# Attention feeding a mixture of experts: query chunks of 512, 512, 320 and 512, and a new place for the first block's join

## The chip, the cores and the metric

The kernel runs on one core of one Trainium2 chip. The metric is the device time of one execution in microseconds (us); less is better. The core's engines are the matrix engine PE (its weight loads are shown apart as PEld), the vector engine DVE, the scalar engine ACT, GpSimd (POOL) and SyncE (SP), which here issues nearly all DMAs in one queue, in order. Each engine also works in order.

## The reference

Attention without softmax over 8 batches of 1856 rows is followed by a mixture of 16 experts, in which each row goes to one expert:

```python
scores = scale * np.matmul(z, z.transpose(0, 2, 1))   # z: (8, 1856, 64), scale = 1/1856
attn = np.maximum(scores, 0.0) ** 2
x = u * np.matmul(attn, v)                             # u, v: (8, 1856, 256)
...
g_logits = x @ w_group                                 # 4 groups, the best one is taken
e_logits = xg @ w_expert[g]                            # 4 experts in it, the best one is taken
h = np.maximum(xg[mask_e] @ w1[g, e], 0.0)             # 256 -> 1024
ye = h @ w2[g, e]                                      # 1024 -> 256
out[tok_idx] = combined[:, None] * ye                  # weight of group times weight of expert
```

All data are fp32. The kernel splits each operand into a high and a low part and adds three products, so a "product" below is up to three matmuls.

## The kernel before, in words

**Attention.** A batch's 1856 queries are cut into four chunks of `QW` = 512, 512, 416 and 416 columns, beginning at `QO`. For each chunk there are 15 key steps (14 of 128 keys and one of 64). A step is named (batch, chunk, key step) here, so (7,3,4) is the fifth key step of the last chunk of the last batch. `scores` makes two matmuls of the chunk's width into one of three score banks; ACT takes relu (L330) and square (L336; in key steps 4 and 10 ACT squares twice, L333 and L334), DVE rounds to the high part `ah` (L337) and subtracts to the low part `al` (L340). `attn_v` then adds six matmuls of the chunk's width (L357, L358, L360) to two accumulators. `scores` runs five steps (`LEAD`) ahead of `attn_v`.

**End of a chunk.** `chunk_end` multiplies the accumulators with `ut` (`xT`, L378), splits the result into `xh` and `xl` (L379, L380), and copies it in 16-bit planes into `pl` (L398). Four or five steps later SP issues one DMA transpose for each 128 rows of the chunk (`rows<-pl`, L404), PE makes the router's logits (L414, L415), ACT copies them (`lgp`, L419), SP transposes them (`lgx`, L422), and DVE copies them back (`lgf`, L428) and works through the routing in some 25 small instructions, among them `base` (L542), the running count of rows of each expert. All matmuls of routing share one bank, so the logits of a chunk wait until `base` of the chunk before has been read out of it. POOL scatters the rows to a DRAM buffer, `bucket`, one call for each 128 rows (L552). A chunk whose width is no multiple of 128 has a part tile, with copies and memsets of its own.

**Handing over to the experts.** While the last batch runs, SP issues 16 `fill`s (L640, L641): each writes `NPAD` padding rows of 1056 bytes into `bucket` behind the rows that an expert has after (6,2). It reads the place from `cbi`, which DVE writes after that chunk's routing. The scatter of (6,3) comes after all fills. The first expert's weights are loaded at `E0_LOADS` (`raw_e`, L175 and L184) and split at `E0_CUTS` (ACT L179 and L191, DVE L180 and L192). The rows of the first block of 512 are read back from `bucket` at the first step of `X0_LOADS` (`xp`, L696, and `meta`, L699) and joined at `X0_JOINS`: DVE merges `meta` (L725) and copies `xf` (L710), ACT makes `xh_m` (L716), DVE `xl_m` (L718). The second block is loaded at the second step of `X0_LOADS`.

**Experts.** The blocks of up to 512 rows run one after another: `up` (L735 to L737, then L740 on ACT and L741 on DVE) and `down` (L751 to L753), all in an order written out by hand.

**Order.** The tables give program steps in which an instruction is written down. After the first 15 steps, a scheduler with a timeline of its own then orders the attention's instructions on each engine, so an instruction can stand some steps away from its step.

Of the kernel before, what the change touches and what calls it, by code (L numbers as in the profile page):

```python
# [19 lines left out]
P = 128  # L20
# [4 lines left out]
def f32(ap):  # L25
    return ap.bitcast(F32)
# [3 lines left out]
def tile_glu_attn_moe(  # L30
# [12 lines left out]
    B, D, S = uT.shape  # L43
# [7 lines left out]
    NK = NKF + 1  # L51
    assert TAIL == 64 and DQ == 64 and ND == 2 and NE == 16
    NQ = 4
    QW = [512, 512, 416, 416]
    QO = [0, 512, 1024, 1440]
    ZW = [512, 512, 512, S - 1536]
    assert sum(QW) == S
    assert all(cv % 16 == 0 and cv >= 2 * P for cv in caps)
    RW = D + 8
# [10 lines left out]
    ACT_TWICE = (4, 10)  # L70
    NT = 4
    NEARLY = 2
    NPAD = 3 * P
    FRZ = min(512, min(caps[:NEARLY]))
    assert min(caps[:NEARLY]) > FRZ or len(set(caps)) == 1

# [5 lines left out]
    def sb(tag, shape, dt, bufs, name):  # L82
        return pool.tile(shape, dt, tag=tag, bufs=bufs, name=name)

    def cst(name, shape, dt=F32):
        return pool.tile(shape, dt, tag=name, bufs=1, name=name)
# [23 lines left out]
    views = dram_disjoint_views(bucket, B * NQ * NT + NE)  # L110

    padrow = cst("padrow", [P, RW], I32)
# [58 lines left out]
    def load_w(e, wt, piece, name):  # L171

        raw = new_stg(f"raw_{name}_{piece}")
        if piece < 2:
            nc.sync.dma_start(raw, w1[ds(e, 1), piece * P:(piece + 1) * P, :].rearrange("o p f -> p (o f)"))  # L175

            def split():
                hi, lo = wt["h"][piece], wt["l"][piece]
                held(nc.scalar.copy(out=hi, in_=raw))  # L179
                nc.vector.tensor_sub(out=lo, in0=raw, in1=f32(hi))  # L180
        else:
            q = piece - 2
            rv = raw.rearrange("p (a d) -> p a d", d=D)
            nc.sync.dma_start(  # L184
                rv, w2[ds(e, 1), q * 4 * P:(q + 1) * 4 * P, :].rearrange("o (a p) d -> p (o a) d", p=P)
            )

            def split():
                for j in range(2):
                    t = wt["2"][2 * q + j].rearrange("p (a t d) -> p a t d", a=2, t=2)  # L190
                    held(nc.scalar.copy(out=t[:, :, 0, :], in_=rv[:, 2 * j:2 * j + 2, :]))  # L191
                    nc.vector.tensor_sub(out=t[:, :, 1, :], in0=rv[:, 2 * j:2 * j + 2, :], in1=f32(t[:, :, 0, :]))  # L192

        return split
# [84 lines left out]
    def prep_zm(b, c):  # L279
        zm = sb("zm", [P, 512], F32R, 2, f"zm_{b}_{c}")  # L280
        q = QO[c]
        while q < QO[c] + QW[c]:
            n = min(512 * (q // 512 + 1), QO[c] + QW[c]) - q
            z2h, z2l = bz[(b, q // 512)]
            src, dst = slice(q % 512, q % 512 + n), slice(q - QO[c], q - QO[c] + n)
            nc.vector.tensor_copy(out=zm[0:DQ, dst], in_=f32(z2h[0:DQ, src]))
# [33 lines left out]
    def scores(s):  # L320
        b, c, k = steps[s]
        w = QW[c]
        z2h, z2l = bz[(b, k // 4)]
# [22 lines left out]
    def attn_v(s):  # L346
# [6 lines left out]
        for d in range(ND):  # L353
            d0 = (k % 4) * D + d * P
            dsl = slice(d0, d0 + P)
            o = oa[d][:, 0:QW[c]]
            nc.tensor.matmul(o, vl[:, dsl], ah, start=(k == 0), stop=False)  # L357
# [4 lines left out]
    def load_ut(b, c):  # L362
        w = QW[c]
        t = sb("ut", [P, ND, 512], F32, 2, f"ut_{b}_{c}")[:, :, 0:w]
        nc.sync.dma_start(t, uT[b, :, QO[c]:QO[c] + w].rearrange("(d p) q -> p d q", p=P))
        ut[(b, c)] = t

    def chunk_end(s):
# [8 lines left out]
        for d in range(ND):  # L377
# [4 lines left out]
        nc.gpsimd.iota(rows[:, 0:nt, D + 1:RW], pattern=[[P, nt], [0, RW - D - 1]],  # L382
                       base=b * S + QO[c], channel_multiplier=1)
        part = w % P
# [253 lines left out]
    def fill(e):  # L638

        r = nc.sync.value_load(cbi[0:1, e:e + 1], min_val=0, max_val=NROW - NPAD)  # L640
        ins = nc.sync.dma_start(  # L641
            views[B * NQ * NT + e][ds(r, NPAD), :].rearrange("(p t) w -> p t w", p=P),
            padrow.unsqueeze(1).to_broadcast([P, NPAD // P, RW]),
        )
        filled.append(ins)

# [30 lines left out]
    def regs(j):  # L677
        while not is_sorted:
            run_gens(NS, 1)
        if j not in ereg:  # L680
            ereg[j] = nc.sync.value_load(eli[0:1, j:j + 1], min_val=0, max_val=NE - 1)
            rreg[j] = nc.sync.value_load(rli[0:1, j:j + 1], min_val=0, max_val=(NE - 1) * CAPB)
        return ereg[j], rreg[j]
# [20 lines left out]
    def load_rows(i):  # L704
        j, r0, n = blocks[i]
        rows_b[i] = load_x(i, regs(j)[1] + r0, n)
# [14 lines left out]
    def join_block(i):  # L721
        j, r0, n = blocks[i]
        xp, meta = rows_b[i]
        nt = (n + P - 1) // P
        nc.vector.tensor_tensor(  # L725
            out=meta[:, 0:nt, 1], in0=meta[:, 0:nt, 1], in1=none[:, j, r0 // P:r0 // P + nt], op=ALU.max
        )
        yield from join_x(i, xp, n)
# [164 lines left out]
        ("v", 0, (0, 1), (0, 6)), ("v", 1, (0, 7), (0, 12)), ("v", 2, (0, 13), (1, 4)), ("v", 3, (1, 5), (1, 10)),  # L893
        ("z", 0, (1, 7), (1, 13)), ("z", 1, (2, 5), (2, 11)), ("z", 2, (3, 5), (3, 11)), ("z", 3, (3, 6), (3, 13)),
    )
    E0_LOADS = ((1, 4), (1, 5), (1, 10), (1, 14))
    E0_CUTS = ((1, 9), (1, 13), (2, 5), (2, 8))
    E1_LOADS = ((2, 9), (2, 13), (3, 7), (3, 11))
    E1_CUTS = ((3, 6), (3, 9), (3, 13))
    X0_LOADS = ((2, 3), (3, 4))  # L900
    X0_JOINS = ((2, 10), (2, 11), (2, 12))
    xs = []
    x0 = []
    e0_cuts = []
# [2 lines left out]
    def step(s):  # L907
# [8 lines left out]
        if b + 1 == B:  # L916
            if (c, k) in E0_LOADS:
                e0_cuts.append(load_w(regs(0)[0], wts[0], E0_LOADS.index((c, k)), "e0"))
            if (c, k) in E0_CUTS:
                e0_cuts[E0_CUTS.index((c, k))]()  # L920
            if (c, k) in E1_LOADS:
                wts.setdefault(1, {"h": [], "l": [], "2": []})
                e1_cuts.append(load_w(regs(1)[0], wts[1], E1_LOADS.index((c, k)), "e1"))
            if (c, k) in E1_CUTS:
                pc = E1_CUTS.index((c, k))
                add_w(wts[1], pc, "e1")
                e1_cuts[pc]()
            if (c, k) in X0_LOADS:
                load_rows(X0_LOADS.index((c, k)))
            if (c, k) == X0_JOINS[0]:  # L930
                x0.append(join_block(0))
            if (c, k) in X0_JOINS:
                xs[:] = [next(x0[0])]
# [10 lines left out]
        if len(filled) < NE and s == NS - NQ * NK + 1 + len(filled) * 7 // 4:  # L944
            fill(len(filled))
# [226 lines left out]
    with order:  # L1172
        for g in range(NB * NF):
            i, f = divmod(g, NF)
            e, r0, n = blocks[i]
# [26 lines left out]
            if i >= OLD:  # L1202
                if f == 2 and i > OLD:
                    p = i - 1
# [5 lines left out]
        e, r0, n = blocks[i]  # L1210
# [42 lines left out]
```

## Time and profile before

| | |
|---|---|
| median of 3 runs | 1535.82 us (1535.66 to 1537.08) |
| the profiled execution's own time | 1536.54 us |
| its span in the profile | 1534.8 us |
| granted PE clock, mean | 0.997 |
| attention, from the first matmul of `attn_v` to the last | 9 to 842 us |
| matmuls of 512 and of 416 columns in attention | 1888 and 1888 |

Rows of a timeline give the start, the duration, the engine, the line and the tiles of an instruction. In square brackets stands the engine's idle time before it and what ended it. Matmuls overlap: the time that one costs is the distance to the next one's start, not its duration.

### The profile page before, as it was taken

What the parts mean: (1) busy time and instruction counts of PE and PEld (TensorE: products, weight loads), DVE (VectorE), ACT (ScalarE), POOL (GpSimd) and SP (SyncE); (2) the same over time, 40 slices, a digit from 0 to 9 for tenths busy, and PEclk for the clock granted to TensorE, in tenths of its full rate; (3) what the DMA queues carried; (4) which work ended last, traced back from release to release, by engine and by line L of the source; (5) the groups of instructions that cost most, each with busy time, mean ns of one, the idle gap of its engine ahead of it and who ended that gap; (6) DMA issues with size and microseconds to landing.
All of it is one profiled execution on the core that took longest, in us unless ns stands there. A gap on an engine that the chain in (4) does not pass through costs nothing. (4 is left out here: it accounts for less than half of the span.)

```text
span 1534.8 us, 23216 instructions
## 1 busy us (share of the span) xinstructions
PE 1519.0 (99%) x7527; PEld 1338.9 (87%) x7527; DVE 1118.4 (73%) x2676; ACT 999.4 (65%) x1896; POOL 293.5 (19%) x356
## 2 busy tenths in 40 slices
PE   9999999999999999999999999999999999999998
PEld 7898988988989989889888799998888888888887
DVE  7888878888888888788887658765655566666663
ACT  8888788878888888788886444444444444444442
POOL 0013121211221121212112231211221222221112
PEclk9999999999999999999999999999999999999999
DMA  4334333323333243333545344554444445454430
GB/s 136 102 74 126 83 85 104 86 76 102 87 105 84 70 112 84 79 87 87 166 157 120 91 114 116 133 115 125 112 118 115 125 118 133 128 131 126 126 97 30
DMA packets 301995, 163.51 MB, mean 107 GB/s; under 512 B 240027, under 2 KB 283043, under 8 KB 301872
## 3 DMA queue, kind: packets, MB, share of 16 engines
q1 hardware_dynamic: 289568, 130.72, 34.4%
q0 software_dynamic: 11952, 30.90, 6.3%
q8 instruction: 59, 0.97, 0.3%
q14 instruction: 64, 0.52, 0.1%
q10 hardware_dynamic: 352, 0.39, 0.1%
HBM read 72.50 MB, written 38.45 MB: 72 GB/s over the span
## 5 line engine op out<-in xcount | busy, mean ns | idle before, releaser
L740 ACT ACTIVATE hh<-ph 128x512 fp32r<-128x512 f32 (+10 forms) x288 | 156.1, 542 | 349.6 <-PE ph L737 342.9
L357 PE MATMUL o<-ah,vl 128*128 128x512 f32 (+1 forms) x960 | 357.3, 373 | 3.0 <-DVE ah L337 2.8
L358 PE MATMUL o<-ah,vh 128*128 128x512 f32 (+1 forms) x960 | 357.2, 372 | 0.0
L741 DVE SCALAR_TENSOR_TENSOR hl<-ph,hh 128x512 fp32r<-128x512 f32 (+10 forms) x288 | 177.3, 616 | 223.7 <-ACT hh L740 182.5
L340 DVE TENSOR_TENSOR al<-r,ah 128x512 fp32r<-128x512 f32 (+1 forms) x448 | 286.4, 640 | 66.9 <-ACT r L334 49.7
L330 ACT ACTIVATE r<-sc 128x512 f32<-128x512 f32 (+1 forms) x480 | 257.5, 552 | 97.0 <-PE sc L328 83.5
L360 PE MATMUL o<-al,vh 128*128 128x512 f32 (+1 forms) x896 | 281.0, 373 | 0.4 <-DVE al L340 0.4
L336 ACT ACTIVATE r<-r 128x512 f32<-128x512 f32 (+1 forms) x416 | 238.7, 591 | 5.2
L552 POOL DMA_INDIRECT bucket<-rows,di x128 | 138.7, 1083 | 485.3 <-DVE al L340 177.4
L756 POOL DMA_INDIRECT out_dram<-yf,meta x121 | 124.0, 1025 | 511.1 <-DVE yf L795 483.3
L737 PE MATMUL ph<-xl_m,w1h_e 128*128 128x512 f32 (+10 forms) x576 | 208.0, 361 | 0.0
L736 PE MATMUL ph<-xh_m,w1h_e 128*128 128x512 f32 (+10 forms) x576 | 207.8, 361 | 0.0
L735 PE MATMUL ph<-xh_m,w1l_e 128*128 128x512 f32 (+10 forms) x576 | 207.5, 360 | 0.0
L357 PEld LDWEIGHTS o<-ah,vl 128*128 128x128 f32 x960 | 181.1, 189 | 22.8 <-DVE ah L337 3.3
L358 PEld LDWEIGHTS o<-ah,vh 128*128 128x128 f32 x960 | 181.2, 189 | 18.8
L753 PE MATMUL y<-hl,w_e 128*128 128x512 f32 (+9 forms) x544 | 196.3, 361 | 0.3 <-DVE hl L741 0.3
L752 PE MATMUL y<-hh,w_e 128*128 128x512 f32 (+9 forms) x544 | 196.1, 360 | 0.0
L751 PE MATMUL y<-hh,w_e 128*128 128x512 f32 (+9 forms) x544 | 196.0, 360 | 0.0
L360 PEld LDWEIGHTS o<-al,vh 128*128 128x128 f32 x896 | 167.5, 189 | 18.1 <-DVE al L340 1.3
L337 DVE CAST ah<-r 128x512 fp32r<-128x512 f32 (+1 forms) x416 | 168.4, 405 | 19.3 <-ACT r L336 17.8
L327 PE MATMUL sc<-zm,z2h 128*128 128x512 f32 (+1 forms) x480 | 179.7, 374 | 0.8 <-ACT r L330 0.8
L328 PE MATMUL sc<-zm,z2l 128*128 128x512 f32 (+1 forms) x480 | 178.6, 372 | 0.0
(170 smaller groups left out, 2088.9 us busy)
## 6 DMA issues: line engine op xcount, KB each, us to landing
raw_e<-in_w_dram SPq DMA_DIRECT2D x64, 512.0 KB
vr<-in_v_dram SPq DMA_DIRECT2D x23, 512.0 KB
ut<-in_uT_dram SPq DMA_DIRECT2D x16, 512.0 KB
ut<-in_uT_dram SPq DMA_DIRECT2D x16, 416.0 KB
bucket<-padrow SPq DMA_DIRECT2D x16, 396.0 KB
zr<-in_zT_dram SPq DMA_DIRECT2D x47, 128.0 KB
vr<-in_v_dram SPq DMA_DIRECT2D x9, 256.0 KB
rows<-pl SPq DMA_TRANSPOSE x128
```

What stands on the lines that cost most here:

```text
L330: nc.scalar.activation(out=a, in_=ps[:, 0:w], func=AF.Relu, scale=1.0 / S)
L336: nc.scalar.activation(out=a, in_=a, func=AF.Square)
L340: nc.vector.tensor_sub(out=al, in0=a, in1=f32(ah))
L357: nc.tensor.matmul(o, vl[:, dsl], ah, start=(k == 0), stop=False)
L358: nc.tensor.matmul(o, vh[:, dsl], ah, start=False, stop=(k == NK - 1))
L360: nc.tensor.matmul(o, vh[:, dsl], al, start=False, stop=False)
L735: nc.tensor.matmul(o, wt["l"][d][:, fs], xh[:, d, 0:W], start=(d == 0), stop=False)
L736: nc.tensor.matmul(o, wt["h"][d][:, fs], xh[:, d, 0:W], start=False, stop=False)
L737: nc.tensor.matmul(o, wt["h"][d][:, fs], xl[:, d, 0:W], start=False, stop=(d == ND - 1))
L751: nc.tensor.matmul(o, w2t[:, 1, dsl], hh[:, 0:W], start=(f == 0), stop=False)
L752: nc.tensor.matmul(o, w2t[:, 0, dsl], hh[:, 0:W], start=False, stop=False)
L753: nc.tensor.matmul(o, w2t[:, 0, dsl], hl_[:, 0:W], start=False, stop=(f == NF - 1))
```

## The change

The query chunks become 512, 512, 320 and 512 wide. The fills write 416 rows instead of 384, from 104 partitions with four rows each instead of 128 with three. The first expert's third and fourth weight pieces are loaded two and one steps later, and its first, second and fourth piece are split two, one and one steps later. The first block's rows are loaded two steps later and joined in the last chunk, at key steps 3 to 5, instead of the third chunk, at key steps 10 to 12; the second block's rows are loaded four steps later.

```diff
-    QW = [512, 512, 416, 416]
-    QO = [0, 512, 1024, 1440]
+    QW = [512, 512, 320, 512]
+    QO = [0, 512, 1024, 1344]
...
-    NPAD = 3 * P
+    PADP = 104
+    NPAD = 4 * PADP
...
-            views[B * NQ * NT + e][ds(r, NPAD), :].rearrange("(p t) w -> p t w", p=P),
-            padrow.unsqueeze(1).to_broadcast([P, NPAD // P, RW]),
+            views[B * NQ * NT + e][ds(r, NPAD), :].rearrange("(p t) w -> p t w", p=PADP),
+            padrow[0:PADP].unsqueeze(1).to_broadcast([PADP, NPAD // PADP, RW]),
...
-    E0_LOADS = ((1, 4), (1, 5), (1, 10), (1, 14))
-    E0_CUTS = ((1, 9), (1, 13), (2, 5), (2, 8))
+    E0_LOADS = ((1, 4), (1, 5), (1, 12), (2, 0))
+    E0_CUTS = ((1, 11), (1, 14), (2, 5), (2, 9))
...
-    X0_LOADS = ((2, 3), (3, 4))
-    X0_JOINS = ((2, 10), (2, 11), (2, 12))
+    X0_LOADS = ((2, 5), (3, 8))
+    X0_JOINS = ((3, 3), (3, 4), (3, 5))
```

One line more stands ahead of the rest, so L725 of before is L726 of the change, and so on.

What the tables do to the order is seen on the engines. First DVE, around the first block's join. Before, `al_10837` is the low part of step (7,3,1) and `ah_10853` the high part of (7,3,2):

```order
L340 TENSOR_TENSOR al_10837<-r_10832,ah_10834 128x416
L481 TENSOR_TENSOR key_1_10710<-key_1_10710,iota_78 128x80
L725 TENSOR_TENSOR meta_10626<-meta_10626,none 128x4
L487 TENSOR_REDUCE sm_1_10731<-ex_1_10708 128x20
L710 COPY xf_10803<-xp_10624 128x2x2x512
L484 TENSOR_REDUCE km_1_10729<-key_1_10710 128x20
L337 CAST ah_10853<-r_10851 128x416
```

In the change, `al_10798` is the low part of (7,3,3) and `al_10822` that of (7,3,4), whose high part ACT makes:

```order
L341 TENSOR_TENSOR al_10798<-r_10793,ah_10795 128x512
L485 TENSOR_REDUCE km_1_10652<-key_1_10633 128x20
L508 RECIPROCAL sm_1_10654<-sm_1_10654 128x20
L491 TENSOR_TENSOR oh_1_10677<-key_1_10633,km_1_10652 128x80
L726 TENSOR_TENSOR meta_10590<-meta_10590,none 128x4
L711 COPY xf_10906<-xp_10588 128x2x2x512
L497 TENSOR_TENSOR oh_7_1_10680<-oh_1_10677 128x64
L519 TENSOR_TENSOR sel_1_10741<-sm_1_10654,oh_1_10677 128x16
L511 COPY pre_1_10722<-oh_7_1_10680 128x16
L523 TENSOR_REDUCE ew_1_10744<-sel_1_10741 128x4
L515 TENSOR_TENSOR pre_1_10722<-pre_1_10722,oh_7_1_10680 128x16
L341 TENSOR_TENSOR al_10822<-r_10817,ah_10819 128x512
```

The join has moved back by two steps on DVE, and it stands behind `xT` and `xl` of chunk (7,2) instead of ahead of them.

Second, SP's queue where the first block's rows are read back (`lgx_1` and `rows_1` belong to chunk (7,1)). Before:

```order
L422 DMA_TRANSPOSE lgx_1_10562<-lgp_1_10561 128x8x48
L696 ISA
L696 DMA_TRANSPOSE xp_10624<-bucket 128x4x512
L699 ISA
L699 DMA meta_10626<-bucket 128x4x2
L404 DMA_TRANSPOSE rows_1_10558<-pl_1_10560 128x4x128 x4
```

In the change:

```order
L423 DMA_TRANSPOSE lgx_1_10483<-lgp_1_10482 128x8x48
L405 DMA_TRANSPOSE rows_1_10479<-pl_1_10481 128x4x128 x4
L697 ISA
L697 DMA_TRANSPOSE xp_10588<-bucket 128x4x512
L700 ISA
L700 DMA meta_10590<-bucket 128x4x2
```

The four transposes of chunk (7,1) have moved ahead of the two reads.

Third, SP's queue at the first expert's first weights (`raw_e_0`, `raw_e_1`). Before, the last three of the 16 fills stand behind them:

```order
L175 ISA
L175 DMA raw_e_0_10259<-in_w_dram 128x1024
L175 ISA
L175 DMA raw_e_1_10277<-in_w_dram 128x1024
L640 TENSOR_LOAD cbi
L640 ISA x2
L641 ISA
L641 DMA bucket<-padrow 384x1x264
```

In the change the last fill stands ahead of `ut`, of the transposes of chunk (7,0) and of the weights:

```order
L642 DMA bucket<-padrow 416x1x264
L366 DMA ut_2_10033<-in_uT_dram 128x2x320
L405 DMA_TRANSPOSE rows_0_10022<-pl_0_10024 128x4x128 x4
L423 DMA_TRANSPOSE lgx_0_10026<-lgp_0_10025 128x8x48
L682 TENSOR_LOAD eli
L682 ISA x2
L683 TENSOR_LOAD rli
L683 ISA x2
L176 ISA
L176 DMA raw_e_0_10182<-in_w_dram 128x1024
```

So all fills are ahead of the weights. Of the 16, two still stand ahead of the transposes of chunk (6,3) and 14 behind its `lgx`, as a block.

Three more moves are told in words. DVE's `cbi` stands behind `al` of (7,0,4), before it stood behind `ah` of (7,0,7). DVE's `lgf` of chunk (6,3) stands behind `al` of (7,0,10), before behind `al` of (7,0,12), and ACT's exponential of that routing stands ahead of the relu of (7,0,13), before ahead of that of (7,1,0). ACT's split of the first weight piece stands behind the square of (7,2,0), before behind that of (7,1,13).

## The prediction

> **What bounds the kernel now.** I read the page first: which engine fills the span.
>
> ```profile
> PE 1519.0 (99%) x7527; PEld 1338.9 (87%) x7527; DVE 1118.4 (73%) x2676; ACT 999.4 (65%) x1896; POOL 293.5 (19%) x356
> ```
>
> PE is the bound, so an edit pays only if it makes matmuls cheaper or takes a PE wait away. Next the timeline of PE, for starts that lie further apart than one matmul costs. The longest such place is in the last batch, at the first block's join. Rows of PE, DVE, POOL and SP:
>
> ```profile
> 813.26 0.54 PE L360 MATMUL o<-al,vh 128*128 128x416 f32 x2
> 816.20 0.72 PE L357 MATMUL o<-ah,vl 128*128 128x416 f32 x1 [2.40 <-DVE ah L337]
> 819.71 0.35 PE L327 MATMUL sc<-zm,z2h 128*128 128x416 f32 x1
> ...
> 813.91 0.17 DVE L725 TENSOR_TENSOR meta<-meta,none 128x4 int32<-128x4 int32 x1 [1.92 <-DMA meta<-bucket]
> 814.14 1.29 DVE L710 COPY xf<-xp 128x2048 uint16<-128x2048 uint16 x1
> 815.47 0.68 DVE L337 CAST ah<-r 128x416 fp32r<-128x416 f32 x1
> ...
> 802.13 1.01 POOL L552 DMA_INDIRECT bucket<-rows,di  x1 [6.66 <-DVE di L548]
> 809.29 0.17 POOL L382 IOTA rows<- 128x28 int32 x1 [1.37 <-DMA bucket<-rows,di]
> ...
> 804.02 1.23 SPq L422 DMA_TRANSPOSE lgx<-lgp  x1
> 809.32 2.11 SPq L696 DMA_TRANSPOSE xp<-bucket  x1
> 812.11 5.12 SPq L404 DMA_TRANSPOSE rows<-pl  x4
> ```
>
> The scatter of chunk (7,0) lands at 809.3, the reads start there, `meta` lands 4.6 us later, DVE has waited 1.92 us for it, and `ah` of (7,3,2) stands behind the join. PE stands still for 2.4 us. Then it is slow: 10 matmuls fill 816.20 to 819.71, 3.51 us, where 188.3 ns each (below) would make 1.88. The whole place costs 2.56 + 1.63 = 4.2 us.
>
> Two smaller waits stand near: for the first expert's weights, and for the last chunk's logits.
>
> ```profile
> 776.81 0.96 SPq L175 DMA_DIRECT2D raw_e<-in_w_dram  x2
> 780.64 1.05 ACT L179 CAST w1h_e<-raw_e 128x1024 fp32r<-128x1024 f32 x1 [4.79 <-DMA raw_e<-in_w_dram]
> 782.24 0.46 PE L327 MATMUL sc<-zm,z2h 128*128 128x416 f32 x1 [0.83 <-ACT r L330]
> ...
> 847.88 1.28 DVE L192 TENSOR_TENSOR w_e<-raw_e,w_e 128x512 fp32r<-128x512 f32 x2
> 849.52 0.43 PE L414 MATMUL pl<-xh,whl 128*128 128x416 f32 x1 [1.77 <-DVE base L542]
> ```
>
> They cost some 1.0 and 1.9 us. All else is matmul time.
>
> **The change part by part.** *Widths.* First and last rows of runs without a gap: 416 columns in attention (86 matmuls between the starts), 512 in attention (88), 320 in an expert block (71).
>
> ```profile
> 589.22 0.35 PE L327 MATMUL sc<-zm,z2h 128*128 128x416 f32 x1
> 605.41 0.54 PE L360 MATMUL o<-al,vh 128*128 128x416 f32 x2
> ...
> 222.91 0.39 PE L327 MATMUL sc<-zm,z2h 128*128 128x512 f32 x1
> 242.88 0.39 PE L357 MATMUL o<-ah,vl 128*128 128x512 f32 x1
> ...
> 902.75 0.31 PE L735 MATMUL ph<-xh_m,w1l_e 128*128 128x320 f32 x1
> 913.16 0.31 PE L753 MATMUL y<-hl,w_e 128*128 128x320 f32 x1
> ```
>
> That is 16.19/86 = 188.3 ns, 19.97/88 = 226.9 and 10.41/71 = 146.6. Two matmuls of 416 cost 376.6 ns, one of 512 and one of 320 cost 373.5. A chunk has 118 matmuls and 4 of logits, so 8 x 122 pairs save 3.1 ns each: -3.0 us. Ends: 0 (nothing shows 320 columns in attention) and -4.
>
> *Do ACT and DVE keep up at 320 columns?*
>
> ```profile
> L330 ACT ACTIVATE r<-sc 128x512 f32<-128x512 f32 x240 | 138.4, 592 | 51.4 <-PE sc L328 46.2 <-DVE al L340 2.4 <-DVE ah L337 1.0
> L330 ACT ACTIVATE r<-sc 128x416 f32<-128x416 f32 x240 | 119.1, 512 | 45.6 <-PE sc L328 37.3 <-issue 1.4 <-DVE ah L337 1.1
> L337 DVE CAST ah<-r 128x512 fp32r<-128x512 f32 x208 | 88.5, 425 | 9.1 <-ACT r L336 7.8 <-issue 0.6 <-ACT r L330 0.6
> L337 DVE CAST ah<-r 128x416 fp32r<-128x416 f32 x208 | 80.0, 384 | 10.2 <-ACT r L336 10.0
> L340 DVE TENSOR_TENSOR al<-r,ah 128x512 fp32r<-128x512 f32 x224 | 155.0, 692 | 44.6 <-ACT r L334 38.0 <-ACT r L336 3.2
> L340 DVE TENSOR_TENSOR al<-r,ah 128x416 fp32r<-128x416 f32 x224 | 131.4, 587 | 22.3 <-ACT r L334 11.7 <-ACT ah L333 6.6 <-ACT r L336 1.7
> 476.40:499.70 23.30, 23.30 (x126) 22.46 (x125) 18.48 (x57) 19.89 (x40) 5.21 (x7) 1.00 0.33 81
> ```
>
> The last row is an undisturbed chunk of 416, (4,2): 23.3 us, DVE busy for 18.5 and ACT for 19.9. From 512 to 416 columns relu loses 80 ns, the rounding `ah` 41 and `al` 105, so I let them lose as much again to 320. With square like relu, 15 steps take 2.4 us from ACT; 14 `al` and 13 `ah` take 2.0 from DVE. PE's chunk loses about 41.7 ns in 108 matmuls and gains 38.6 in the 10 scores of the next chunk: 19.2 us. ACT would be busy for 17.5 of 19.2 (91%, before 85%) and DVE for 16.5 (86%, before 79%), with the end of a chunk of 512 among it. Score banks and the five steps' lead buffer bursts of some 3 us, so I take no wait of weight: +0.5 us over all batches, ends 0 and +4 (0.5 a batch). The dearer step of 512 in the last chunk has room. Fewer part tiles, memsets and scatters lie beside PE: nothing.
>
> *The join.* The anchors are the first matmul of the last step of chunk (7,1), just behind which chunk (7,2) begins, and the first expert's wait, used further down:
>
> ```profile
> 780.79 0.61 PE L360 MATMUL o<-al,vh 128*128 128x512 f32 x2
> 787.36 0.39 PE L357 MATMUL o<-ah,vl 128*128 128x512 f32 x1
> ```
>
> In the change SP first issues `lgx` of (7,1), then four transposes (5.12 us in the row above), then the reads. Before, `lgx` stood at 804.02, 16.6 us after this anchor; ACT saves up to 2.1 of its 2.4 us by then, so I take 14.5 to 16.6. With 1.2 for `lgx` itself, 5.1 for the transposes and 4.6 up to the landing, `meta` is there 25.4 to 27.5 us after the anchor. PE begins the last step of (7,2) some 19.2 us after the anchor, and is at (7,3,4) another 7.0 us on (four steps of 8 x 226.9 ns are 7.3; the first of them mixes in matmuls of 320): at 26.2. That step's `al` is due four matmuls later, at 27.1. After `meta`, DVE needs 0.1 + 1.2 + 0.5 of routing + 0.6 for that `al`, so it is ready at 27.8 to 29.9. PE waits for 0.7 to 2.8 us; I take 1.3, as ACT's lead makes the earlier end likelier. A wait near the upper end, the length of that before, could bring the slow spell too. Gain 4.2 - 1.3 = -2.9; ends -4.2 and 0. If the reads' cover is gone, `al` of (7,3,4) is late next.
>
> *Weights and fills.* Rows of SP and DVE:
>
> ```profile
> 740.10 0.17 DVE L594 CAST cbi<-base 128x16 int32<-128x16 f32 x1
> 741.33 2.43 SPq L641 DMA_DIRECT2D bucket<-padrow  x2
> 746.93 1.22 SPq L422 DMA_TRANSPOSE lgx<-lgp  x1
> 749.73 0.35 DVE L428 COPY lgf<-lgx 128x320 uint16<-128x320 uint16 x1 [2.07 <-DMA lgx<-lgp]
> 752.55 11.86 SPq L641 DMA_DIRECT2D bucket<-padrow  x9
> 744.56 0.69 DVE L340 TENSOR_TENSOR al<-r,ah 128x512 fp32r<-128x512 f32 x1 [1.57 <-ACT r L336]
> 748.59 0.60 ACT L330 ACTIVATE r<-sc 128x512 f32<-128x512 f32 x1 [0.55 <-PE sc L328]
> q1 hardware_dynamic: 2948, 2.95, 71.5%
> ```
>
> A fill takes 11.86/9 = 1.32 us of SP. The last row is the DMA view of 752 to 764 us (packets, MB, share of 16 engines): 71.5% busy, so a longer fill can hide in SP's spacing up to 1/0.715, and 8% more rows do. `cbi` is ready about two steps earlier less what stands ahead of it, some 1.7 us. SP issues two fills, four transposes and `lgx` by some 749.5, 14 fills by 768.5 to 770.5, `ut`, four transposes, `lgx` and the register loads, and the weights at 777 to 779, before 776.8. They land 3.8 us later, at 781 to 783. ACT splits them two steps later than before, and the score that needs the relu behind them comes at 784.4 instead of 781.2 (where the row of 780.79 ends PE's work before), since in PE's order 12 matmuls of 512 and some of 320 lie between; 1.45 us after the landing is 782.3 to 784.2. So the wait of 1.0 goes: -0.8, ends -1.0 and +1.5.
>
> By the Trainium skill's "DMA: Bandwidth & Descriptors", section on why a DMA increments its semaphore by 16, a transfer uses the largest number of engines up to 16 that divides its outer dimension: 16 for 128 partitions, 13 for 104. By that rule a fill would keep 13 engines busy 416/384 x 16/13 = 1.33 times as long, 1.26 us for 0.94 (0.715 x 1.32), just under the 1.32 of its issue: the sum would stay, and the rival on fills below would be avoided by 5%. The trace does not name a packet's engine.
>
> *A new wait.* `lgf` of (6,3) now stands two steps earlier on DVE, behind `al` of (7,0,10) (the row of 744.56), and the exponential behind it stands on ACT ahead of relu (7,0,13). Before, `lgf` waited for 2.07 us without a wait of PE. Now DVE comes to it at 745.2 and `lgx` lands at 750.4 to 751.2. Relu (7,0,13) can start 2.0 us after the landing and be done 0.6 us later. PE's scores of (7,0,14) end at 748.6, where the ACT row follows them; those of (7,1,1), which need relu (7,0,13)'s bank, come 17 matmuls, 3.9 us, later: 752.5. PE waits for 0.5 to 1.3: +0.8, ends 0 (the cover before was whole) and +2.
>
> *Last chunk's logits.* They wait until `base` of (7,2) is read. The pair of splits (1.28 us) that stood ahead of it now stands before `xT`, and PE has three matmuls more (0.7 us) to do first; the wider `xT` and `xl` take 0.4 longer. Of 1.9 I leave 1.0: -0.9, ends -1.9 and +1.0.
>
> Sum: -3.0 + 0.5 - 2.9 - 0.8 + 0.8 - 0.9 = -6.3 us against the span of 1534.8, which lies 1.7 below that execution's own time of 1536.5, which is 0.7 above the median of 1535.8. So the median comes to 1529.5.
>
> **The rivals.**
> *The join only moves its wait* (no change or little gain): `meta` lands at 27.5 or later, because four transposes now stand ahead of it. PE then waits 2.5 us and runs 1.6 us slow; so the gain of 2.9 is gone down to 0.1; with the widths at nothing besides, -0.5 is left: 1535.3. For it speaks that SP's queue is the longer one; against it that PE needs the rows two steps, 3.6 us, later.
> *The narrow chunk starves* (slower): ACT's relu comes later than the score banks bear, in each batch, from 20.5 us of ACT work in a chunk of 19.2 on. At 20.7, 1.5 us in each of eight batches, this gives +12 for +0.5, so 1529.5 + 11.5 = 1541. For it: the four copies of 1.0 and 0.6 us at a chunk's end come in a row. Against it: 85% busy without a PE gap before.
> *Fills hold the queue*: if a fill's time goes with the rows of one partition, four for three, 1.32 us become 1.76, 14 take 6 us more, `lgx` of (7,0) and the weights land at 787 to 789, and PE waits 4.5 us and runs 1.6 slow: the gain of 0.8 becomes a loss of 6.1, 1529.5 + 6.9 = 1536.4.
> *The widths pay nothing, the waits go*: 1529.5 + 3.0 = 1532.5. For it speaks that no row has 320 columns in attention; against it the straight fall from 226.9 at 512 to 146.6 at 320.
>
> **How the numbers follow.** Forecast 0.56, its own range 1526 to 1532.7; the widths without gain 0.16; the join's wait stays 0.11; fills 0.08; starving 0.09. A measurement tells about 0.2%, 3.1 us, from no change: faster means below 1532.7, slower above 1538.9. Faster: 0.56 + 0.16 = 0.72. Same: 0.11 and 0.08, with rounding 0.18. Slower: about 0.10. The low end takes the gains at their ends without the join's last microsecond, 1525; the high end reaches to the first and third rival, 1536.
>
> **What would show it.** The matmuls of 512 and 320 at 227 and 147 ns in attention, and PE in (4,2) without rows in brackets: the widths. PE at step (7,3,4) with a wait below 2 us, and no slow spell: the join. `raw_e` without a long bracket on ACT that PE repeats: the weights. A bracket on PE near 753: the new wait. The sum is wrong if brackets on PE appear in each batch's third chunk, or if rows of fills stand 1.7 us apart.

## The result, and the profile after

The change makes the kernel slower: 1554.7 us (1553.35 to 1557.8) against 1536.26 in the same comparison, a ratio of 1.0123 with a 95% interval of 1.0105 to 1.014. Forecast were 1529.5 us, a range of 1525 to 1536, and a chance of about 0.10 for slower.

The page's line on the engines, of the change:

```profile
PE 1515.8 (98%) x7527; PEld 1300.2 (84%) x7527; DVE 1119.4 (72%) x2644; ACT 1002.4 (65%) x1872; POOL 276.5 (18%) x332
```

PE works 3.2 us less than before, as the new widths let one expect, in a span of 1551.6 instead of 1534.8. So the loss is a wait. PE's timeline shows it in the second of these rows:

```profile
777.46 0.62 PE L361 MATMUL o<-al,vh 128*128 128x512 f32 x2
799.82 0.80 PE L358 MATMUL o<-ah,vl 128*128 128x512 f32 x1 [21.74 <-DVE ah L338]
800.41 0.63 PE L359 MATMUL o<-ah,vh 128*128 128x512 f32 x1
```

PE stands still for 21.7 us at the end of chunk (7,1), and the next rows come 0.43 us apart for some 3 us, in place of 0.23. The bracket names `ah`; who held it up is seen on DVE, ACT and SP in the same stretch:

```profile
799.10 0.35 DVE L429 COPY lgf<-lgx 128x320 uint16<-128x320 uint16 x1 [22.84 <-DMA lgx<-lgp]
...
800.61 0.44 ACT L331 ACTIVATE r<-sc 128x320 f32<-128x320 f32 x1 [22.99 <-DVE al L341]
...
803.84 1.05 ACT L180 CAST w1h_e<-raw_e 128x1024 fp32r<-128x1024 f32 x1 [2.29 <-DMA raw_e<-in_w_dram]
...
737.10 6.01 SPq L405 DMA_TRANSPOSE rows<-pl  x4
743.21 1.21 SPq L423 DMA_TRANSPOSE lgx<-lgp  x1
745.83 43.29 SPq L642 DMA_DIRECT2D bucket<-padrow  x14
789.22 0.46 SPq L366 DMA_DIRECT2D ut<-in_uT_dram  x1
789.90 6.04 SPq L405 DMA_TRANSPOSE rows<-pl  x4
796.04 1.21 SPq L423 DMA_TRANSPOSE lgx<-lgp  x1
799.45 0.94 SPq L176 DMA_DIRECT2D raw_e<-in_w_dram  x2
```

Read from the bottom: the 14 fills hold SP's queue until 789. Behind them stand the transposes and `lgx` of chunk (7,0) and the first expert's weights. DVE has come to `lgf` of that chunk at 776 and waits there, with the attention's `ah` and `al` behind it in its order; ACT and PE run dry one after the other. Not the weights stop the kernel first, but the router's logits one row ahead of them; the weights cost ACT another 2.3 us.

A fill takes much more of SP than before. The fills' rows among the instructions that touch `bucket`, of before and then of the change (ns shortest, median, longest, then first and last start):

```profile
L641 SPq DMA_DIRECT2D bucket<-padrow x16: 547/554/693, 741.3 to 781.9; - x16
```

```profile
L642 SPq DMA_DIRECT2D bucket<-padrow x16: 953/960/1125, 731.9 to 788.2; - x16
```

The issue itself went from 0.55 to 0.96 us. From 745.83 to the last start at 788.2 the fills stand 3.26 us apart, where 1.32 were expected. Most of the rest is the next fill's register load of `cbi`, which the rows above leave out: in the trace's records it takes 0.3 to 0.4 us behind most fills of before and 1.73 to 1.95 behind a fill here.

And the DMA view of that stretch in the change:

```profile
DMA packets 5579, 5.74 MB, mean 133 GB/s; under 512 B 169, under 2 KB 5577, under 8 KB 5577
q1 hardware_dynamic: 5577, 5.71, 48.8%
```

The 16 DMA engines are busy for 48.8% here, for 71.5% in before's stretch of 752 to 764 us. So the transfers are not at a limit; the time goes on SP itself.

### The profile page after: what moved, and what is told of

It is laid out like the page before. It is cut to its first block, busy times and chain, and to the rows that moved or that the text cites. A ratio compares the mean times of both kernels' runs of the same rounds, so it can differ in the third digit from the quotient of the medians.

```text
span 1551.6 us, 23124 instructions
## 1 busy us (share of the span) xinstructions
PE 1515.8 (98%) x7527; PEld 1300.2 (84%) x7527; DVE 1119.4 (72%) x2644; ACT 1002.4 (65%) x1872; POOL 276.5 (18%) x332
## 5 line engine op out<-in xcount | busy, mean ns | idle before, releaser
L361 PE MATMUL o<-al,vh 128*128 128x512 f32 (+1 forms) x896 | 295.7, 372 | 0.5 <-DVE al L341 0.5
L553 POOL DMA_INDIRECT bucket<-rows,di x120 | 129.3, 1077 | 566.1 <-issue 239.3
```

Of the source, the lines that this page charges most:

```text
L361: nc.tensor.matmul(o, vh[:, dsl], al, start=False, stop=False)
```

## The experiments

The theory after this reading: a fill is dear when its partition count isn't a multiple of 16, whatever it carries. The rival: four rows a partition, or the longer fill, is dear.

**Fills of 128 partitions with four rows.**

```diff
-    PADP = 104
+    PADP = 128
```

> The change with fills of 512 rows from 128 partitions with four rows each (instead of 416 from 104). Theory P (a fill whose partition count is no multiple of 16 is dear; the change's fills stand 3.25 us apart on SP, before's 1.4): though a third more bytes than before are written, the fills stand 1.4 to 1.9 us apart, the first weights land by 785, PE's wait of 21.9 us is gone, and the time is 1529 to 1534. Theory R (four rows a partition, or the longer fill as such, is what is dear): 3.2 us or more apart, PE still waits some 20 us or more, 1555 to 1565.

Measured 1528.65 us (1528.09 to 1531.63, before 1535.49), ratio 0.9957 (0.9944 to 0.9971). One number of the change makes the difference between 18 us lost and 7 gained. SP's queue now, and the DMA view of 743 to 764.4:

```profile
743.09 21.36 SPq L642 DMA_DIRECT2D bucket<-padrow  x14
764.54 0.59 SPq L366 DMA_DIRECT2D ut<-in_uT_dram  x1
765.35 5.51 SPq L405 DMA_TRANSPOSE rows<-pl  x4
770.96 1.21 SPq L423 DMA_TRANSPOSE lgx<-lgp  x1
775.61 0.46 SPq L176 DMA_DIRECT2D raw_e<-in_w_dram  x2
...
q1 hardware_dynamic: 6576, 6.74, 93.4%
```

The fills carry 23% more rows than the change's and are through in half the time, now at the limit of the DMA engines. This is the change as it was meant, and below it is called the mended change.

**Fills of 120 partitions with four rows** (`PADP = 120`).

> The change with fills of 480 rows from 120 partitions with four rows each. Theory P: 120 is no multiple of 16 either, so the fills stand 3.2 to 3.8 us apart (3.25 times 480/416 at most), time 1554 to 1562. Theory R: about 3.2 to 3.8 as well. If only the number of engines counted (15 of 16 for 120, 13 for 104), they would be at 1.9 or less and the time near 1532.

Measured 1557.99 us (one run), fills 3.30 us apart, issue 0.99. 120 partitions are as dear as 104.

**Fills of 32 partitions with thirteen rows** (`PADP = 32`, `NPAD = 13 * PADP`).

> The change with its 416 rows written from 32 partitions with thirteen rows each. Theory P: 32 is a multiple of 16, so the fills stand 1.3 to 1.6 us apart and the time is 1528 to 1533. Theory R: thirteen rows a partition are dearer than four, so 3.2 us apart or more and 1555 or more.

Measured 1539.77 us (1538.47 to 1542.58), ratio 1.0027 (1.0017 to 1.0037): between the two. The issue is cheap again (0.61 us), but the fills stand 2.2 us apart, with the DMA engines 92% busy (746 to 765 us): a packet of 1056 bytes takes 79 ns in the median, where all other forms so far have 47. Neither theory had that: the forecasts were 1528 to 1533 and 1555 or more. PE waits 8.2 us.

**The kernel before with the change's fills.**

```diff
-    NPAD = 3 * P
+    PADP = 104
+    NPAD = 4 * PADP
...
-            views[B * NQ * NT + e][ds(r, NPAD), :].rearrange("(p t) w -> p t w", p=P),
-            padrow.unsqueeze(1).to_broadcast([P, NPAD // P, RW]),
+            views[B * NQ * NT + e][ds(r, NPAD), :].rearrange("(p t) w -> p t w", p=PADP),
+            padrow[0:PADP].unsqueeze(1).to_broadcast([PADP, NPAD // PADP, RW]),
```

> The kernel before, with the change's fills (104 partitions with four rows) and nothing else of it. Theory P and theory R alike: 13 of the 16 fills stand ahead of the first weights, each 1.85 us longer, so the weights land some 20 us later than at 780.6, PE waits some 17 to 21 us near 781, and the time is 1553 to 1558: the fills alone make the whole loss. Rival (the loss comes from all 16 fills now standing ahead of the weights, and from the later table entries): 1536 to 1542.

Measured 1561.61 us (1560.51 to 1562.29), ratio 1.017 (1.0154 to 1.0185). PE waits here too:

```profile
800.99 0.80 PE L358 MATMUL o<-ah,vl 128*128 128x512 f32 x1 [18.07 <-DVE ah L338]
```

The fills alone do the harm, more than forecast, since smaller waits (0.92 at 758, 1.73 at 806) come on top. In this kernel 13 of the 16 stand ahead of the weights, as before; so it is not the cause that all 16 do in the change.

**Fills of 112 partitions with four rows** (`PADP = 112`, seven times 16).

> The change with fills of 448 rows from 112 partitions (7 x 16) with four rows each. Theory P (a count that is no multiple of 16 is dear): the fills stand 1.4 to 1.65 us apart, as with 128 partitions (1.60), and the time is 1527.5 to 1530. Rival (only the full 128 partitions, or a power of two, is cheap): 3.2 us apart, as with 104 and 120, and 1554 to 1558.

Measured 1530.9 us (1529.05 to 1532.87), ratio 0.9971 (0.9961 to 0.9981); fills 1.67 us apart, issue 0.61. So it is the multiple of 16, not the full 128 and not a power of two. The time is a small miss: PE still waits 1.41 us at 778. The 14 fills begin 1.4 us later than with 128 partitions, behind transposes that take 7.45 us instead of 5.90, and stand a little further apart, so `lgx` of (7,0) is issued at 774.36 instead of 770.96. Packets of the fills take 57 ns in the mean here, against 50 with 128 partitions. Why, no run tells.

**Fills of 8 partitions with 52 rows** (`PADP = 8`, `NPAD = 52 * PADP`).

> The change with its 416 rows written from 8 partitions with 52 rows each, so that 8 engines carry a fill. Theory K (any count of engines below 16 costs SP more): the fill's issue takes about 1 us as with 104 and 120 partitions (0.96 and 0.99; 0.55 to 0.61 with 16 engines). Rival (only a count that is no power of two): 0.6 us or less. Either way a fill's transfer itself is longer, 52 rows an engine at 47 to 80 ns, so they stand 2.5 to 4.5 us apart and the time is 1545 to 1575.

Measured 1651.14 us (one run). Packets take 153 ns here, and the fills stand 7.5 us apart, so the forecast of the time missed by far. Only the first fill, which has no other fill ahead of it, tells the theories apart. For each form, from SP's records: the first fill's issue and the register load that follows it, and the mean distance of the last 14:

| fill | rows | first issue, us | register load after it, us | distance, us |
|---|---|---|---|---|
| before, 128 x 3 | 384 | 0.69 | 0.30 | 1.41 |
| 128 x 4 | 512 | 0.70 | 0.30 | 1.60 |
| 112 x 4 | 448 | 0.76 | 0.30 | 1.67 |
| 32 x 13 | 416 | 0.76 | 0.29 | 2.20 |
| 120 x 4 | 480 | 1.16 | 1.97 | 3.30 |
| 104 x 4 | 416 | 1.12 | 1.95 | 3.26 |
| 8 x 52 | 416 | 0.93 | 2.22 | 7.55 |

(Of before, the distance is that of the nine in a row.) In the third and fourth column together there are two groups, with nothing between: from the first fill's start, multiples of 16 leave SP free after 1.0 to 1.1 us, the others after 3.1 to 3.2. A power of two doesn't help: 8 partitions cost as much.

Then the rest of the change. **Only the widths** (the mended change with both of before's tables).

> The kernel before with the new widths and fills of 512 rows from 128 partitions; the tables of the first expert's weights and of the first block's rows are those of before. Widths worth what the prediction gave them (3.0 us, in the long runs 0.34 a batch by now), the join's wait of 4.2 us kept, weights up to 2.6 us later for 13 fills that are 0.2 us longer each: 1532 to 1537, and the time from one batch to the next falls from 102.9 to 102.5 or 102.6. If the narrow chunk starved, brackets on PE would stand in each batch and the time would be above 1538.

Measured 1535.42 us (1535.02 to 1536.56), ratio 1.0004 (0.9995 to 1.0013). The chunks are cheaper, yet the end does not move. PE:

```profile
778.84 0.41 PE L328 MATMUL sc<-zm,z2h 128*128 128x320 f32 x1 [1.84 <-ACT r L331]
780.20 0.81 PE L361 MATMUL o<-al,vh 128*128 128x512 f32 x2 [0.80 <-DVE al L341]
...
810.34 0.42 PE L358 MATMUL o<-ah,vl 128*128 128x320 f32 x1 [2.68 <-DVE ah L344]
```

Chunk (7,0) begins at 726.5 instead of 730.0, and PE then waits for the weights (2.6 us) and at the join (2.7), each with a slow spell behind it. That lies within the forecast of 1532 to 1537.

**The mended change with the old join.**

```diff
-    X0_LOADS = ((2, 5), (3, 8))
-    X0_JOINS = ((3, 3), (3, 4), (3, 5))
+    X0_LOADS = ((2, 3), (3, 4))
+    X0_JOINS = ((2, 10), (2, 11), (2, 12))
```

> The change with fills of 128 partitions (512 rows), but with the first block's rows loaded and joined where before had them (third chunk, key steps 10 to 12). If the move of the join is worth what the prediction said (2.9 us): 1531 to 1533, with a wait and a slow spell of PE early in chunk (7,3). Rival, the move's gain is given back at the last chunk's logits (there 2.6 us of wait and a slow spell follow in the version with the moved join): 1528 to 1530, and the logits wait below 2 us here.

Measured 1532.05 us (1529.77 to 1533.31), ratio 0.9977 (0.9968 to 0.9986; the interval overlaps a little with the mended change's 0.9944 to 0.9971). The time is that of the first theory and the place that of neither: near the join PE waits only 0.7 us, and the price is paid at the last chunk's logits:

```profile
844.00 0.77 PE L415 MATMUL pl<-xh,whl 128*128 128x512 f32 x1 [4.14 <-DVE df L546]
```

**The mended change with the old weights table** (`E0_LOADS`, `E0_CUTS` of before).

> The change with fills of 128 partitions (512 rows), but with the first expert's weights loaded and split where before had them. If moving them is worth what the prediction gave (0.8 us): 1529 to 1530. Rival, from the pair with the old join (1535.4 without and 1532.1 with the move): about 3 us, since the narrower chunk brings PE to the first split's place earlier than in before: 1531 to 1533.5, with a PE wait of 2 to 4 us at 776 to 781 that the version with the move doesn't have.

Measured 1532.3 us (1531.27 to 1533.49), ratio 0.9981 (0.9972 to 0.999), with waits of 2.01 and 0.80 us at 779 and 781 that the mended change doesn't have. The rival was nearer: by the medians the move is worth 3.65 us, not 0.8. The two traces alone don't show it: their spans are 1529.8 here and 1529.9 in the mended change, whose profiled execution (1531.63 us) is the slowest of its five and pays at the last chunk's logits.

**Before with the new join only** (`X0_LOADS`, `X0_JOINS` of the change).

> The kernel before with only the first block's rows loaded and joined where the change has them. If the move of the join is worth the predicted 2.9 us by itself: 1531.5 to 1533, the wait and the slow spell near 815 gone. Rival, it is given back at the last chunk's logits: 1534 to 1536, with a wait there above 2.5 us (before 1.9).

Measured 1534.54 us (1532.22 to 1536.4), ratio 0.9993 (0.9984 to 1.0002). The wait of 2.4 us at the join is gone, but:

```profile
847.25 0.69 PE L414 MATMUL pl<-xh,whl 128*128 128x416 f32 x1 [3.26 <-DVE base L542]
```

The logits wait 3.26 us instead of 1.77, with a slow spell of 5.8 us behind them.

**Before with both tables.**

> The kernel before with both tables of the change (first expert's weights, first block's rows), but with the old widths and the old fills. By the prediction's terms (join 2.9, weights 0.8, logits 0.9, new wait -0.8): 1531 to 1533. Rival, the tables only pay together with the new widths: 1534 to 1537.

Measured 1534.16 us (1533.01 to 1535.26), ratio 0.9991 (0.9982 to 1.0). No wait at the weights, none at the join, and 3.90 us with a spell at the logits. The rival was nearer.

**The mended change with a later second join.** In it, too, the last chunk's logits wait 2.63 us for `base`. DVE's rows show what stands ahead of `base`:

```profile
840.73 0.68 DVE L742 SCALAR_TENSOR_TENSOR hl<-ph,hh 128x512 fp32r<-128x512 f32 x1
841.33 0.15 DVE L726 TENSOR_TENSOR meta<-meta,none 128x4 int32<-128x4 int32 x1
841.40 0.20 DVE L536 TENSOR_TENSOR rk<-pk,base 128x48 f32<-128x48 f32 x1
841.54 1.31 DVE L711 COPY xf<-xp 128x2048 uint16<-128x2048 uint16 x1
842.74 0.20 DVE L541 TENSOR_TENSOR rk<-rk,oh 128x48 f32<-128x48 f32 x1
842.86 0.17 DVE L543 TENSOR_TENSOR base<-pk,base 128x16 f32<-128x16 f32 x1
...
843.17 0.77 PE L415 MATMUL pl<-xh,whl 128*128 128x512 f32 x1 [2.63 <-DVE base L543]
```

`xf` of the second block (1.31 us) stands between, though nobody needs it yet.

```diff
-                f0 = 4 if i + 1 == NEARLY else 3
+                f0 = 4 if i + 1 <= NEARLY else 3
```

> The change with fills of 128 partitions (512 rows), and with the second block's join begun one step of the first block later (as the third block's already is), so that on DVE the base of (7,2) stands ahead of that join's copy xf (1.3 us) instead of behind it. Theory: the logits' wait of 2.63 us near 842 falls to 1.0 to 1.5, the slow spell behind it goes (another 1.9 us), and the time is 1525 to 1527, from 1528.65. Rival: the second block's rows come too late for its first matmuls, PE waits there instead: 1528 to 1530.

Measured 1527.53 us (1525.17 to 1528.49), ratio 0.9944 (0.9931 to 0.9958). The row in its place:

```profile
842.04 0.47 PE L415 MATMUL pl<-xh,whl 128*128 128x512 f32 x1 [1.42 <-DVE df L546]
```

The wait is down by 1.2 us and the slow spell gone; the profiled spans are 1529.9 and 1526.7. The medians differ by 1.1 us only, less than forecast, and the two intervals overlap: that this wait is shorter is shown by the trace, that this version is the faster one is not settled by the times. Both beat before and the change.

## Why the prediction was wrong, point by point

*Fills: the step that failed.* The prediction let 14 fills take 1.32 us of SP each and said that 8% more rows hide in the spacing. They took 3.26. (Its 1.32 is a little low even for before: the row of 11.86 us ends with the ninth fill's issue, and from start to start it is 1.41.) It bounded the cost by rows and by the share of the DMA engines, the two things that the fill of before shows; what SP itself spends on a fill was taken as fixed, and before has fills of one partition count only. The rival "fills hold the queue" had the mechanism and the place (`lgx` of (7,0) and the weights), but its price came from rows a partition (1.76 us) and it got 0.08. Its 6 us of delay would be 27 with the measured distance.

By the Trainium skill's "DMA: Bandwidth & Descriptors", section on why a DMA increments its semaphore by 16, 104 partitions go to 13 engines. The trace agrees: packets of 4 bytes come 16 a fill before (128 from 753 to 766 us, in which eight fills end) and 13 a fill in the change (169 for thirteen). The cost that the prediction drew from it, 16/13 on the transfer, was the wrong one: 120 partitions, on 15 engines, are as dear as 104. The same section says that the issuing sequencer writes the increments of the unused engines itself; that would fit a cost on SP, though not in proportion: 1, 3 and 8 such writes go with register loads of 1.97, 1.95 and 2.22 us. What SP does in that time, no run shows.

*Widths (-3.0): right in the batches, lost at the end.* One batch that nothing disturbs, (4,0) to (4,3), in windows of before and then of the change (busy us of each engine; a row gives its window and length first):

```profile
sum 102.90, PE 102.90 PEld 90.79 DVE 83.28 ACT 85.89 POOL 19.48; mean PE 25.73 PEld 22.70 DVE 20.82 ACT 21.47 POOL 4.87
```

```profile
474.40:494.50 20.10, 20.10 (x128) 19.14 (x128) 16.43 (x51) 18.29 (x41) 4.84 (x6) 1.00 0.43 99
...
sum 102.60, PE 102.60 PEld 86.14 DVE 85.84 ACT 86.23 POOL 17.50; mean PE 25.65 PEld 21.54 DVE 21.46 ACT 21.56 POOL 4.38
```

That is 0.30 us a batch, 2.4 in eight. Matmuls of 320 stand 146.7 ns apart in attention (46 in 377.66 to 384.26), as in the experts' blocks. The narrow chunk, the row of 474.40, has ACT busy for 18.29 of 20.10, 91% as worked out, and DVE for 82% (86% forecast); no batch before the last shows a wait of PE there: the 0.5 and the rival of starving fall away. But the term is worth this only while the last batch can take it up: with the widths alone nothing is left of it there (1.0004).

*Join (-2.9): size near, in part by luck.* With the mended fills, old join against new, it is 1532.05 - 1528.65 = 3.4 us, but the old join costs that mainly at the logits (4.14 us of wait against 2.63) and not at its own place (0.7). The wait at (7,3,4) is 0.58 us in the mended change, below the 0.7 to 2.8 of the prediction, with no spell:

```profile
812.73 0.73 PE L361 MATMUL o<-al,vh 128*128 128x512 f32 x2 [0.58 <-DVE al L341]
```

Both ends of that sum came later than predicted, and nearly cancel: `meta` was merged 28.1 us behind the anchor (810.12 - 782.0, the last step of (7,1)) instead of 25.4 to 27.5, and PE got to its `al` after 30.1, not 27.1. And part of what the move saves is paid elsewhere: at the logits. In the kernel before, the move alone brought 1.1 us in the medians, with an interval that reaches past 1.

*Weights (-0.8): too small.* Where the fills are cheap the wait goes, and the old table costs 3.65 us more in the new widths (1532.3 - 1528.65). The prediction compared with the wait of before (1.0) and left out that the widths' own gain brings PE there earlier.

*New wait near 753 (+0.8): absent.* The prediction let `cbi` come 1.7 us earlier; in the mended change it comes 9.1 us earlier (730.97, before 740.10). It needs the routing of (6,2), which is now the narrow chunk: (6,3) begins behind it at 699.8, at 706.5 before. So the first two fills and the transposes go out earlier, and `lgx` of (6,3) is issued at 740.83, not at 748. DVE still waits for it, for 1.89 us in the mended change and for 4.58 in the change itself:

```profile
743.36 0.36 DVE L429 COPY lgf<-lgx 128x320 uint16<-128x320 uint16 x1 [1.89 <-DMA lgx<-lgp]
```

```profile
745.81 0.36 DVE L429 COPY lgf<-lgx 128x320 uint16<-128x320 uint16 x1 [4.58 <-DMA lgx<-lgp]
```

PE shows no wait near it in either trace. So the chain from this wait of DVE to PE, which the prediction built, did not hold.

*Logits (-0.9): wrong sign.* 2.63 us of wait and 1.6 of slow spell in the mended change, against 1.9. What the prediction counted on DVE came out: from the start of `xT` to the end of `base` it is 5.75 us instead of 6.75. What it left out is that DVE comes to `xT` late. The last matmul of `attn_v` and the first `xT` behind it, before and in the mended change:

```profile
841.76 0.35 PE L358 MATMUL o<-ah,vh 128*128 128x416 f32 x1
...
842.62 1.08 DVE L378 TENSOR_TENSOR xT<-o,ut 128x416 f32<-128x416 f32 x2
```

```profile
833.71 0.39 PE L359 MATMUL o<-ah,vh 128*128 128x512 f32 x1
...
837.28 1.28 DVE L379 TENSOR_TENSOR xT<-o,ut 128x512 f32<-128x512 f32 x2
```

PE ends attention 8.05 us earlier, DVE begins `xT` only 5.34 us earlier: it works without a gap from 831.6 on, the two splits and the routing of (7,2) among it. The second block's `xf` stands ahead of `base` before, too. The versions with the new join pay between 1.42 and 3.90 us here; that taking the copy `xf` away from there shortens the wait, the last experiment shows; why it is 1.43 with the old weights table and 1.55 in the change itself stays open.

With the fills mended the sum came out nearly right (-6.3 forecast, 1528.65 - 1535.49 = -6.8 in the medians). By place, in the profiles of before and of the mended change: (7,0) begins 3.3 us earlier (726.7, 730.0), the weights' wait of 1.0 is gone, the join costs 0.6 instead of 4.2, and the logits 4.2 (2.6 and 1.6) instead of 1.9; that is -5.6, and the spans differ by 4.9. The profiled execution of the mended change is the slowest of its five, so for the medians this account is some 2 us short. That the sum is near is in part luck: the logits' loss is hidden in it by a gain at the join that is larger than forecast, and by the wait near 753 that never came.

## What to carry to other kernels

Before the partition count of a DMA like these fills is changed, look whether it stays a multiple of 16; if not, price the issuing queue and not only the transfer, and count what stands behind it in that queue, the next register load first. In an order with several waits close behind each other, a term is only worth what the next wait lets through: widths alone and join alone moved nothing that could be measured, both tables about 0.1% (the interval reaches to 1), and all together, with fills of 128 partitions, 0.43%.

## What the runs showed of the hardware

- A fill, a DMA whose place in DRAM comes from a register, costs SP 1.0 to 1.1 us with 32, 112 or 128 partitions, and 3.1 to 3.2 with 8, 104 or 120, the register load behind it included (the first fill of each form). In these forms a multiple of 16 goes with 16 packets of 4 bytes a fill and any other count with fewer (8, 13, 15), so the runs don't tell whether the partitions or the engines count. No run has a DMA with a fixed place in such a form.
- Packets of 1056 bytes out of 128 partitions take 47 ns in the median, out of 32 partitions 79, out of 8 (8 closing packets of 4 bytes a fill) 153.
- PE ran at half rate behind 14 of the 15 waits of 2.40 us and more in these traces (2.40, 2.49, 2.61, 2.63, 2.68, 3.26 and longer), and at full rate behind one of 2.59, at 874 us in the kernel before with the change's fills. Of the shorter waits outside such a spell, one of 1.84 that another of 0.80 follows brought half rate; 2.01 followed by 0.80 did not, nor did single ones of 1.42, 1.77, 1.96 and 2.16. The spells that no further wait cuts into last 3 to 6 us. The Trainium skill's "TensorE: Matmul & The Clock Gate", part 1, has the clock fall back after an idle window of about 3.4 us, which runs freely; the runs show that shorter waits can be enough, and that between 1.8 and 2.6 us the length alone does not decide.
